# Linear attention, top-1 MoE and FFN in one kernel: the first expert unit's rows are all gathered in the attention's drain, and the last three chunks are routed inside that unit

## The chip, the cores and the metric

The kernel runs on one core of one Trainium2 chip. The metric is the device time of one execution in microseconds (us); lower is better. The names of the engines are those of the profile: PE (TensorE; PEld is its weight load), DVE (VectorE), ACT (ScalarE), POOL (GpSimd), and SP (SyncE, which issues most DMAs).

## What is computed

Three layers follow one another. The reference, cut:

```python
# q, k, v: (4, 8, 576, 64); w_phi: (64, 128)
proj = x @ w_phi;  proj -= max(abs(proj), -1);  phi(x) = concat(exp(proj), exp(-proj))
kv = phi(k).T @ v;  z = sum(phi(k));  attn = (phi(q) @ kv) / (phi(q) @ z + 1e-6)   # per head

x = attn as (2304 tokens, 512)
logits = x @ w_gate                         # 8 experts
e = argmax(logits);  g = max(softmax(logits))
# in token order, each expert takes its first 576 tokens (capacity); the rest are dropped
y[token] = g * (relu(x @ w1[e]) @ w2[e])    # w1: (512, 1024), w2: (1024, 512); 0 if dropped

h = y @ w_in                                # (512, 2048)
out = (h - tanh(h)) @ w_out                 # (2048, 512)
```

With the reference's inputs the counts of tokens per expert are 0, 576, 0, 0, 0, 0, 1152, 576, so three experts have work. In the first 1536 tokens they are 576 for expert 1 and 960 for expert 6.

## The kernel before

**Attention.** The 2304 tokens are 18 chunks of 128. One loop over steps s = 0..24 is a software pipeline: step s projects the k of chunk s, adds chunk s-1 to the sum kv (`kv_step`, L347), projects the q of chunk s-5 (`proj`, L304; `sub` at L312 and L315 takes the maximum off on DVE), transposes the q of chunk s-6 (`trans`, L381; ACT takes the exponentials) and multiplies it with kv (`num`, L420). From step 18 on there is no k left; steps 18 to 24 are called the drain here. Besides, w_in and the first part of w_out are unpacked piece by piece in steps 5 to 17 (`cv_*`: L94 on DVE, L98 and L278 on POOL).

**Routing** goes by groups of chunks. `route1` (14 short DVE operations, L448 to L489; the one-hot `oh` of each token's expert is L479) starts when the last chunk of a group has its `num`. `prefix` (PE, L502 to L505) counts the tokens of each expert ahead of each token. `route2` and `table` (DVE, L514 to L558) turn that into a slot per token, and `map_mm` (PE, L576) with `map_add` (L583) add the tokens to a table of slots. The first four groups of three chunks are "paced": their operations are spread over several steps between the large DVE operations of `sub`. The fifth group is (12, 13, 14), and the tail is (15, 16) and (17).

**The experts.** A unit is one expert with up to 576 tokens in six blocks of 96 rows; a row is fetched by an indirect DMA (`xgather`, L862), multiplied by its scale on POOL (`weigh`, L873), transposed on PE and split into a high and a low part (`xsplit`, L882; split at L850 on ACT and L851 on DVE). Every product is three matmuls (high x high, high x low, low x high; L854, L855, L856). A unit has an FF1 phase (eight steps `ff1` -> `relu` -> `ff2`, whose weights come through three raw buffers and are split at L836 on ACT and L841 on DVE) and an FFIN phase (sixteen steps `ffin` -> `gate` -> `ffout`). The result of ff2 is in four PSUM tiles `acc0` to `acc3` and is split into xh, xl by `evac_y`; `ff1` and `ffin` write two tiles `h0` and `h1` in turn. The last six pieces of w_out are unpacked inside unit 0 (`late_load`, `late_bits`, `late_split`): four in its FF1 phase (LF = 4), two in its FFIN phase. Units follow one another in nested branches on the number of experts in use.

**Between the two.** `first_gather` stands ahead of the last-but-one `num`: it finishes the table for 15 chunks, takes the first expert that has a token as unit 0 and gathers its first three blocks as far as these 15 chunks hold them. The last three chunks are not gathered. After the loop they are added by matmuls: `block_rows` (L621) puts the three gathered blocks into four PSUM banks, `block_add` (L627) adds the tokens of chunks 15 to 17 that belong there by a selection matrix (L535), and `x0` splits the four banks into xh and xl. The tail's rows are stored, its table is added, and the three other blocks are gathered when unit 0 begins. All work is issued in the order of the program (a manual schedule): each engine runs its instructions in that order, and an instruction that waits holds those behind it.

## Time and profile before

| | |
|---|---|
| time of three runs | 719.15 us median (717.67 to 719.91) |
| the profiled execution | 717.26 us, of which the span from first to last instruction is 715.4 us |
| mean granted clock of PE | 0.976 of full speed |
| busy share of the span | PE 92%, DVE 75%, ACT 60%, POOL 36% |
| drain's end to unit 0's first matmul | 192.91 to 216.35 us: 23.44 us, PE 14.44 us busy, clock 0.72 |
| FF1 phase of unit 0 | 216.35 to 267.80 us: 51.45 us, PE 50.80 us busy |
| the rest (unit 0's FFIN, two more units) | 267.80 to 715.40 us: 447.6 us, PE 428.79 us busy |

The table of stages is to be read by the difference between a stretch and PE's busy time in it: where the two agree, PE sets the time, and where they don't, a wait does. The granted clock is the share of full speed that TensorE had; a matmul takes about twice as long at 0.50.

### The profile page before, as it was taken

The page shows a single profiled execution, that of the slowest core. Times are in us where ns is not written, and L with a number is a line of the kernel's source. Part 1 is how long each engine was busy: PE and PEld are TensorE (multiplying, and loading weights), DVE is VectorE, ACT ScalarE, POOL GpSimd, SP SyncE. Part 2 cuts the span into 40 slices and gives each one's busy share as a digit, 9 for nine tenths or more (in the row PEclk, how much of TensorE's full clock was granted, in tenths as well). Part 3 has the DMA queues.
Part 4 walks back from the last instruction along what each step waited for, and adds up shares of the span by engine and source line. Part 5 has one row for each costly group of instructions (what it writes and reads, how often), then busy time and mean ns, then how long its engine had stood idle before and what let it go on. Part 6 is the DMA issues. An engine that isn't in the chain of part 4 may idle for free.

```text
span 715.4 us, 17537 instructions
## 1 busy us (share of the span) xinstructions
PE 656.8 (92%) x7148; PEld 636.5 (89%) x7148; DVE 537.2 (75%) x830; ACT 431.1 (60%) x735; POOL 256.4 (36%) x227
## 2 busy tenths in 40 slices
PE   7899788897679999989999999999999999999984
PEld 6789778787569998989999999999999999999983
DVE  4689898988757685888986554788987655788982
ACT  3599887874543675756764444656764544666661
POOL 1044544552224141563362011363462011362461
PEclk9999999998968999999999999999999999999998
DMA  7978677737616650120222550010222550010211
GB/s 179 278 232 286 205 234 228 247 108 212 199 56 191 225 191 1 30 78 1 74 72 68 176 167 20 1 34 1 79 67 91 168 156 15 2 35 1 68 36 37
DMA packets 62155, 81.35 MB, mean 114 GB/s; under 512 B 25792, under 2 KB 35136, under 8 KB 60400
## 3 DMA queue, kind: packets, MB, share of 16 engines
q1 hardware_dynamic: 58736, 71.92, 32.5%
q0 software_dynamic: 2624, 8.13, 4.0%
q8 instruction: 58, 0.95, 0.5%
q14 instruction: 33, 0.27, 0.1%
q10 hardware_dynamic: 704, 0.08, 0.1%
HBM read 67.06 MB, written 13.05 MB: 112 GB/s over the span
## 4 chain that ended last, share of the span: by engine, by line
PE 61%; DVE 16%; DMA 10%; ACT 7%; issue 3%; POOL 2%; SPq 0%; ACTq 0%; DVEq 0%; POOLq 0%
PE h L854 9%; PE acc L855 9%; PE acc L856 9%; PE acc L854 9%; PE h L856 9%; PE h L855 9%; DMA out<-row,ids 6%; DVE d L315 3%; DVE m L312 3%; PE xb L304 2%; PE kvb L347 1%; DMA raw<-win 1%; PE kvb L420 1%; POOL w_in_l L278 1%; ACT a L85 1%
## 5 line engine op out<-in xcount | busy, mean ns | idle before, releaser
L944 POOL TENSOR_SCALAR al<-ut 128x576 fp32r<-128x576 f32 (+1 forms) x51 | 83.0, 1627 | 148.9 <-ACT ut L940 107.6
L854 PE MATMUL h<-xh,w_in_h 128*128 128x288 f32 x384 | 115.0, 299 | 1.4 <-ACT ut L940 1.4
L855 PE MATMUL h<-xl,w_in_h 128*128 128x288 f32 x384 | 113.3, 295 | 0.0
L856 PE MATMUL h<-xh,w_in_l 128*128 128x288 f32 x384 | 113.0, 294 | 0.0
L841 DVE TENSOR_TENSOR w<-raw,w 128x512 fp32r<-128x512 f32 x98 | 68.0, 712 | 41.0 <-ACT w L836 36.5
L836 ACT CAST w<-raw 128x512 fp32r<-128x512 f32 x98 | 59.1, 620 | 53.6 <-DMA raw<-w 22.6
L939 ACT COPY hs<-h 128x576 f32<-128x576 f32 (+1 forms) x51 | 31.3, 614 | 94.5 <-DVE th L955 63.8
L854 PEld LDWEIGHTS h<-xh,w_in_h 128*128 128x128 f32 x384 | 72.0, 188 | 1.5 <-ACT ut L940 1.5
L854 PE MATMUL acc<-ah,w_oa_h 128*128 128x288 f32 x240 | 71.0, 296 | 2.0 <-ACT ah L931 2.0
L855 PE MATMUL acc<-al,w_oa_h 128*128 128x288 f32 x240 | 71.1, 296 | 1.6 <-DVE al L932 1.6
L856 PEld LDWEIGHTS h<-xh,w_in_l 128*128 128x128 f32 x384 | 72.3, 188 | 0.0
L855 PEld LDWEIGHTS h<-xl,w_in_h 128*128 128x128 f32 x384 | 72.1, 188 | 0.0
L856 PE MATMUL acc<-ah,w_oa_l 128*128 128x288 f32 x240 | 70.7, 294 | 0.0
L932 DVE TENSOR_TENSOR al<-y,ah 128x576 fp32r<-128x576 f32 (+1 forms) x51 | 41.3, 810 | 33.8 <-ACT ah L931 30.3
L984 POOL DMA_INDIRECT out<-row,ids x18 | 21.2, 1180 | 119.9 <-DVE row L982 69.7
L854 PE MATMUL h<-xh,w 128*128 128x288 f32 x192 | 58.7, 306 | 1.1 <-DVE al L900 1.1
L312 DVE TENSOR_REDUCE m<-xb 128x8 f32<-128x1024 f32 x33 | 40.2, 1219 | 24.2 <-PE xb L304 24.1
L855 PE MATMUL h<-xl,w 128*128 128x288 f32 x192 | 57.3, 299 | 0.0
L856 PE MATMUL h<-xh,w 128*128 128x288 f32 x192 | 57.2, 298 | 0.0
L854 PE MATMUL acc<-ah,w 128*128 128x288 f32 x192 | 56.7, 295 | 0.0
L856 PE MATMUL acc<-ah,w 128*128 128x288 f32 x192 | 56.6, 295 | 0.0
L855 PE MATMUL acc<-al,w 128*128 128x288 f32 x192 | 56.5, 294 | 0.0
(223 smaller groups left out, 1901.9 us busy)
## 6 DMA issues: line engine op xcount, KB each, us to landing
raw<-w SPq DMA_DIRECT2D x98, 256.0 KB, 3.0
raw<-win SPq DMA_DIRECT2D x8, 1024.0 KB, 7.0
raw<-wout SPq DMA_DIRECT2D x5, 1024.0 KB, 5.4
k<-kT SPq DMA_DIRECT2D x18, 256.0 KB
vt<-vT SPq DMA_DIRECT2D x18, 256.0 KB, 6.0
q<-qT SPq DMA_DIRECT2D x18, 256.0 KB, 6.1
out<-zero SPq DMA_DIRECT2D x18, 256.0 KB, 3.6
v<-v SPq DMA_DIRECT2D x16, 256.0 KB, 5.4
```

Source lines behind the costliest of these rows:

```text
L304: nc.tensor.matmul(ps[:, g, hp * DF:(hp + 1) * DF], src[64 * g:64 * g + 64, hp * P:(hp + 1) * P], wphi[64 * g:64 * g + 64], start=(hp == 0 ...
L312: nc.vector.tensor_reduce(out=m, in_=ps, axis=AX.X, op=ALU.max, apply_absolute_value=True)
L315: nc.vector.tensor_tensor(out=t, in0=ps, in1=m.unsqueeze(2).to_broadcast([P, H, DF]), op=ALU.subtract)
L836: nc.scalar.copy(d[:, 0], t)
L841: eng.tensor_tensor(out=d[:, 1], in0=t, in1=d[:, 0].bitcast(F32), op=ALU.subtract)
L854: nc.tensor.matmul(o, ah, bh, start=first, stop=False, skip_group_check=True)
L855: nc.tensor.matmul(o, ah, bl, start=False, stop=False, skip_group_check=True)
L856: nc.tensor.matmul(o, al, bh, start=False, stop=last, skip_group_check=True)
L932: nc.vector.tensor_tensor(out=AL[a][:, i], in0=y2[:, i], in1=AH[a][:, i].bitcast(F32), op=ALU.subtract)
L939: nc.scalar.copy(hs[:, i], h[:, i, 0:BLK])
L944: nc.gpsimd.tensor_scalar(out=AL[a][:, i], in0=ut[:, i], scalar1=C2, scalar2=None, op0=ALU.is_gt)
L984: ins = nc.gpsimd.indirect_dma_start(out=out[:, :], out_offset=bass.IndirectOffsetOnAxis(ap=ids[j % 2][0:RCH, rc:rc + 1], axis=0), in_=r[0 ...
```

## The change

- All groups have three chunks. Three are paced, the tail is (15, 16, 17). The group (9, 10, 11) is called `known`: its whole `route1` stands at step 17 in one piece, its `prefix` at step 18 ahead of `kv_step(17)`, its `table` in step 18.
- `first_gather` moves from step 23 to step 19. It chooses as unit 0 the expert with the most tokens in the first 12 chunks (`first_unit`, eight DVE operations in place of four; `had` keeps that count, at most 576). Its blocks 0 to 2 are gathered, weighed, and split by `xsplit` through PSUM bank `kvb[:, 2]` in steps 21 to 23, three weight pieces are split there too, and blocks 3 to 5 are gathered there. `block_rows`, `block_add`, `x0` and the matrix L535 are gone. `ff1(0)` follows the last `num`.
- The tail's `route1`, `prefix`, `route2`, `table`, `map_mm` and the list of the other units (`rest_units`) run inside unit 0, in its steps 0 to 3.
- At the end of unit 0's FF1 phase, `settle` compares the tokens that the chosen expert got in the end with `had` (`more1`). If more came, a branch gathers the six blocks again and repeats FF1 (`redo`); else nothing is done. With the counts above, `had` and the final count both meet the cap of 576.
- PSUM has the same tiles in the whole program: `acc` is the three banks of `kvb`, one tile, and `sb`; `ff1` and `ffin` write `xb` and `yb` in turn.
- Three late pieces of w_out stand in unit 0's FF1 phase and three in its FFIN phase (LF = 3, LO = 4). The four extra weight transfers into unit 0's free buffers are gone.

The diff, cut to its core:

```diff
-    NL = 3
+    NK = 12
+    sb = psp.tile([P, 512], F32, name="sb")
+    kvb = psp.tile([P, 3, 512], F32, name="kvb")
+    xb, yb = (psp.tile([P, 2, 512], F32, name=n) for n in ("xb", "yb"))
+    acc = [kvb[:, 0], kvb[:, 1], kvb[:, 2], sb]
+    hp_ = [xb, yb]
...
-        groups = [tuple(range(c, c + 3)) for c in range(0, NCH - NL, 3)] + [(NCH - 3, NCH - 2), (NCH - 1,)]
-        tailg = groups[-2:]
-        paced = groups[:4]
+        groups = [tuple(range(c, c + 3)) for c in range(0, NCH, 3)]
+        known, tailg = groups[NK // 3 - 1], groups[-1]
+        paced = groups[:3]
...
         def first_gather():
-            map_mm(maps[-1])
-            for _ in itertools.chain(map_add(maps[-1]), map_ids(), first_unit()):
-                pass
-            mo["first"]()
+            map_mm(known)
+            count_mm()
+            run(map_add(known), map_ids(), first_unit())
+            mo["first"](uroom)
...
-            if jn == NCH - 2:
+            if s == SK:
                 first_gather()
...
+            if s >= SK:
+                mo["drain"](s - SK)
+        tail = [lambda: rgen.update(t=route1(tailg)), lambda: run(itertools.islice(rgen["t"], 5)),
+                lambda: run(rgen["t"]), lambda: prefix(tailg, False),
+                lambda: (run(route2(tailg), table(tailg)), flush()),
+                lambda: (map_mm(tailg, False), count_mm(False)),
+                lambda: run(map_add(tailg), map_ids(), rest_units())]
...
-        LF = 4
-        LO = 3
+        LF = 3
+        LO = 4
...
+            if j == 0:
+                settle(aq[n1 - 1])
...
+        def settle(last):
+            with tc.If(nact[1] > 0):
+                redo(last)
...
+        def drain(s):
+            if s in (1, 2, 3):
+                weigh()
+                wcast()
+                wfetch(*((1, 1), (1, 1), (0, 1))[s - 1])
+            if s in (2, 3, 4):
+                xsplit(s - 2, kvb[:, 2])
+                early(s + 1)
```

Three places show in the order of instructions what moved. The names are those of the program's tiles: `d` is q after `sub`, `kp` and `qp` are the exponentials of k and q, `kvs` the sum kv in SBUF, `oh` the one-hot, `idc` and `idd` the table of slots, `few` and `key` small vectors of the choice of the unit.

On PE in step 18, before:

```order
L381 MATMUL yb<-ident,d 128x128 x8
L347 MATMUL kvb<-v_157,kp 64x74 x32
L304 MATMUL xb<-wphi,q 128x128 x8
L420 MATMUL kvb<-kvs_165,qp 64x74 x32
L576 LDWEIGHTS ta
```

and now:

```order
L382 MATMUL yb<-ident,d 128x128 x8
L494 LDWEIGHTS tri
L494 MATMUL sb<-oh,tri 128x24
L496 LDWEIGHTS ones
L496 MATMUL sb<-oh,ones 128x16
L496 LDWEIGHTS ones
L496 MATMUL sb<-oh,ones 128x8
L497 LDWEIGHTS ones
L497 MATMUL sb<-cum,ones 128x24
L348 MATMUL kvb<-v_156,kp 64x74 x32
L305 MATMUL xb<-wphi,q 128x128 x8
L423 MATMUL kvb<-kvs_164,qp 64x74 x32
```

The prefix of chunks 9 to 11, which waits for DVE's `oh`, now stands between the transposes of q and the last `kv_step`.

On DVE between the `sub` of q chunk 13 and that of chunk 14, before:

```order
L315 TENSOR_TENSOR d<-xb,m 128x1024
L448 TENSOR_SCALAR r<-dl 128x24
L449 RECIPROCAL r<-r 128x24
L458 TENSOR_TENSOR lgx<-dl,r 128x192
L462 TENSOR_REDUCE lg<-lgx 128x24
L465 TENSOR_REDUCE mx<-lg 128x3
L468 TENSOR_TENSOR ls<-lg,mx 128x24
L312 TENSOR_REDUCE m<-xb 128x8
```

and now the last eleven of the 26 rows that stand there, with the `sub` behind them (ahead of them are one `idc`, the nine operations of `route2` and `table`, and five on `idc`, `idd` and `idt`):

```order
L595 SCALAR_TENSOR_TENSOR key<-sb,few 128x8
L597 TENSOR_REDUCE few<-key 128x1
L599 TENSOR_SCALAR few<-key,few 128x8
L601 TENSOR_TENSOR key<-few 128x8
L603 TENSOR_REDUCE few<-key 128x1
L605 TENSOR_SCALAR reg_69<-few 1x1
L607 TENSOR_SCALAR few<-few 128x1
L610 TENSOR_SCALAR few<-few 128x1
L125 TENSOR_SCALAR few<-few 128x8
L127 TENSOR_TENSOR uroom<-idt,few 96x48
L130 TENSOR_REDUCE ids_72<-uroom 96x6
L313 TENSOR_REDUCE m<-xb 128x8
```

Six operations of `route1` stood there; now the whole choice of the unit does, behind a table that itself waits for PE.

On PE at the start of unit 0, before (`h_3137` is the first of the two h tiles):

```order
L576 MATMUL sb<-tb,ta 96x98
L780 LDWEIGHTS ones
L780 MATMUL sb<-cum,ones 128x8
L854 MATMUL h_3137<-xh_2500,w_0_2504 128x288
L855 MATMUL h_3137<-xl_2501,w_0_2504 128x288
L856 MATMUL h_3137<-xh_2500,w_0_2504 128x288
```

and now, from the last three `num` and `xsplit` on:

```order
L423 MATMUL kvb<-kvs_165,qp 64x74 x32
L868 MATMUL kvb<-ident,row_2545 128x96 x4
L423 MATMUL xb<-kvs_165,qp 64x74 x32
L840 MATMUL yb<-xh_2533,w_0_2537 128x288
...
L842 MATMUL yb<-xh_2533,w_1_2538 128x288
L868 MATMUL xb<-ident,row_2543 128x96 x4
L840 MATMUL yb<-xh_2533,w_2_2539 128x288
```

The first matmul of the unit follows the last `num`, and the second `ff1` (the last row) writes the tile yb that the first one wrote, since the `xsplit` between them takes xb.

## Rows read from the trace of the kernel before

**Rows 1.** Windows by stage: length, then busy us (and instructions) by engine, clock.
```profile
192.91:216.35 23.44, 14.44 (x58) 11.52 (x58) 12.87 (x50) 11.62 (x38) 6.67 (x11) 0.72 0.37 117
216.35:267.80 51.45, 50.80 (x372) 50.51 (x372) 37.54 (x71) 29.85 (x58) 18.06 (x18) 0.96 0.62 198
```

**Rows 2.** Timeline of PE, drain to unit: start, duration, line, operation, idle before.
```profile
155.24 2.27 PE L347 MATMUL kvb<-v,kp 128*64 128x74 f32 x64
...
167.11 1.94 PE L381 MATMUL yb<-ident,d 128*128 128x128 f32 x8 [3.68 <-DVE d L315]
...
174.03 1.09 PE L381 MATMUL yb<-ident,d 128*128 128x128 f32 x8
...
181.60 1.16 PE L304 MATMUL xb<-wphi,q 64*128 64x128 f32 x16
...
214.81 0.40 PE L576 MATMUL sb<-tb,ta 128*96 128x98 bf16 x2 [3.88 <-DVE ta L558]
...
216.35 0.59 PE L854 MATMUL h<-xh,w 128*128 128x288 f32 x1
...
220.10 0.43 PE L854 MATMUL h<-xh,w 128*128 128x288 f32 x1
```

**Rows 3.** Timeline of POOL in step 18, the unpacking beside route1.
```profile
157.19 2.14 POOL L98 TENSOR_TENSOR a<-a,m 128x1024 f32<-128x1024 f32 x1 [2.89 <-DVE a L94]
...
160.49 2.36 POOL L278 TENSOR_TENSOR w_oa_l<-a,w_oa_h 128x1024 fp32r<-128x1024 f32 x1 [0.52 <-ACT w_oa_h L275]
```

**Rows 4.** Timeline of DVE in the drain.
```profile
158.65 1.23 DVE L312 TENSOR_REDUCE m<-xb 128x8 f32<-128x1024 f32 x1 [1.54 <-PE xb L304]
...
161.05 1.83 DVE L448 TENSOR_SCALAR r<-dl 128x24 f32<-128x24 f32 x1
...
164.49 1.22 DVE L312 TENSOR_REDUCE m<-xb 128x8 f32<-128x1024 f32 x1
...
178.76 0.18 DVE L448 TENSOR_SCALAR r<-dl 128x24 f32<-128x24 f32 x1
...
181.19 0.18 DVE L479 TENSOR_TENSOR oh<-e,mx 128x24 bf16<-128x24 f32 x1
...
185.38 0.17 DVE L514 TENSOR_TENSOR pos<-sb,oh 128x24 f32<-128x24 f32 x1
...
187.46 0.46 DVE L558 TENSOR_TENSOR ta<-slot,pt 128x288 bf16<-128x288 f32 x1
188.36 0.25 DVE L583 TENSOR_TENSOR idc<-idc,sb 96x98 f32<-96x98 f32 x1 [0.44 <-PE sb L650]
...
190.53 0.20 DVE L122 TENSOR_REDUCE ids<-uroom 96x6 int32<-96x48 f32 x1
```

**Rows 5.** Timeline of unit 0's FF1 phase: DVE's relu part, PE's only wait.
```profile
222.37 0.76 DVE L900 SCALAR_TENSOR_TENSOR al<-h,ah 128x576 fp32r<-128x576 f32 x1 [1.45 <-ACT ah L899]
...
235.34 0.52 PE L882 MATMUL h<-ident,row 96*128 96x96 f32 x4 [0.65 <-issue]
```

**Rows 6.** Timeline of PE and DVE at the branch after the last unit.
```profile
696.44 0.37 PE L854 MATMUL acc<-ah,w_ob_h 128*128 128x288 f32 x1 [2.02 <-ACT th L946]
...
702.88 0.46 DVE L932 TENSOR_TENSOR al<-y,ah 128x288 fp32r<-128x288 f32 x1 [2.56 <-issue]
```

**Rows 7.** Timeline of PE's wait by a late piece of w_out in FFIN.
```profile
302.60 0.40 PE L855 MATMUL acc<-al,w_oa_h 128*128 128x288 f32 x1 [0.44 <-DVE al L932]
```

**Rows 8.** Timeline of a split of four PSUM banks: one tile (drain), four tiles (unit 0).
```profile
211.41 0.40 ACT L850 CAST xh<-kvb 128x288 fp32r<-128x288 f32 x1 [0.53 <-DVE xl L851]
...
277.81 1.56 DVE L851 TENSOR_TENSOR xl<-acc,xh 128x288 fp32r<-128x288 f32 x4
...
281.90 0.40 PE L854 MATMUL acc<-ah,w_oa_h 128*128 128x288 f32 x1 [0.95 <-ACT ah L931]
...
604.96 0.40 PE L854 MATMUL acc<-ah,w_oa_h 128*128 128x288 f32 x1 [0.49 <-ACT ah L931]
```

More of the change, by code (lines that the diff above doesn't have):

```diff
@@ L624, in block_add @@
-        def block_add(c):
-            for d in range(4):
-                nc.tensor.matmul(acc[d][:, 0:BLK], xt[c][:, d * P:(d + 1) * P], ohu[c],
-                                 start=False, stop=(c == NCH - 1), skip_group_check=True)
+            nc.vector.tensor_tensor(out=key, in0=one1, in1=wu, op=ALU.mult)
+            yield
+            nc.vector.tensor_reduce(out=reg1f, in_=key, axis=AX.X, op=ALU.max)
+            yield
+            nc.vector.tensor_scalar(out=reg1, in0=reg1f[0:1], scalar1=-1.0, scalar2=64.0, op0=ALU.mult, op1=ALU.add)
@@ L658, in flush @@
                 late.pop(0)()
-        for s in range(NCH + LAG + 2):
+        for s in range(LAST + 1):
             i, j, jt = s, s - LAG, s - LAG - 1
@@ L750, in attention @@
                                   in_=zero.unsqueeze(1).to_broadcast([P, 4, P]))
-            mo["after"](s)
-            if jn == NCH - 2:
-                xscale(NCH - 3)
-        prefix(tailg[0])
-        xscale(NCH - 2)
-        weave([], [route1(tailg[1]), route2(tailg[0])])
-        xscale(NCH - 1)
-        mo["highs"]()
-        block_rows(range(3))
-        block_add(NCH - 3)
-        prefix(tailg[1])
-        block_add(NCH - 2)
-        weave([], [route2(tailg[1])])
-        block_add(NCH - 1)
@@ L1189, in unit, with redo, piece @@
             return [aq2[n2 - 2], aq2[n2 - 1]]
+        def redo(last):
+            idload(0, hs[:, 0])
+            for rc in range(6):
+                xgather(0, rc)
+                weigh()
+                xsplit(rc)
+            spare = next(w for w in W2 if all(w is not x for x in w2q))
+            def piece(fc, half, d):
+                t = nxt("w", rawt)
+                wdma(0, fc, half, t)
+                wpend.pop()
+                nc.scalar.copy(d[:, 0], t)
+                nc.vector.tensor_tensor(out=d[:, 1], in0=t, in1=d[:, 0].bitcast(F32), op=ALU.subtract)
+                return d
+            pend = list(w2q)
+            for b, p in [(b, p) for b in range(2) for p in range(NP1)]:
+                for i in range(2):
+                    w1q.append(piece(2 * p + i, 0, W1[i]))
+                h = ff1(b)
+                if (b, p) == (1, NP1 - 1):
+                    relu(h, last)
+                    break
+                a = relu(h, 1 - last)
+                for i in range(2):
+                    w = piece(2 * p + i, 1, spare)
+                    for d in range(4):
+                        mm3(acc[d][:, 0:BLK], w[:, 0, d * P:(d + 1) * P], w[:, 1, d * P:(d + 1) * P],
+                            AH[a][:, i, :], AL[a][:, i, :], p == 0 and i == 0, p == NP1 - 1 and i == 1)
+                if p == NP1 - 1:
+                    evac_y(b)
+            assert pend == w2q and not w1q and not wpend
+        def settle(last):
+            if G > 1:
+                redo(last)
+                return
+            with tc.If(nact[1] > 0):
+                redo(last)
         def chain(j, prev):
@@ L1211, in after, with first @@
                     nc.gpsimd.memset(r[0:RCH], 0.0)
-        def first():
+        def first(room):
+            for r in rows:
+                nc.gpsimd.memset(r[0:RCH], 0.0)
             use(0)
-            idload(0, mo["room"])
+            idload(0, room)
             wfetch(0, 3)
             for rc in range(3):
-                xgather(0, rc, False, NT - NL * P)
-            weigh(3)
-        def highs():
-            for _ in range(3):
-                wcast_high()
-        def beside():
-            for half in (1, 1, 0):
-                wcast_low()
-                wfetch(half, 1)
@@ L1230, in x0 @@
-        def x0(acc):
-            for d in range(4):
-                split(xh[0][:, d, :], xl[0][:, d, :], acc[d][:, 0:BLK])
-        mo.update(beside=beside, highs=highs, alloc=alloc, after=after, first=first, x0=x0)
-        attention()
-        psp = ctx.enter_context(tc.tile_pool(name="psp", bufs=1, space=bass.MemoryType.PSUM, reuse_waits="tile"))
-        acc = [psp.tile([P, 512], F32, name=f"acc{i}") for i in range(4)]
-        hp_ = [psp.tile([P, 2, 512], F32, name=f"h{i}") for i in range(2)]
@@ L1266, in experts @@
+        mo.update(alloc=alloc, first=first, drain=drain)
+        attention()
+        mq = ctx.enter_context(tc.tile_pool(name="mq", bufs=1, side="right"))
+        W2 += [mq.tile([P, 2, 512], F32R, name=f"w2_{i}") for i in range(NW)]
+        AH += [mq.tile([P, 2, BLK], F32R, name=f"ah{i}") for i in range(2)]
+        AL += [mq.tile([P, 2, BLK], F32R, name=f"al{i}") for i in range(2)]
+        lord = list(range(NOA, 16))
+        tail = mo["tail"]
         chain(0, None)
```

308 lines of the change are left out of this document (143 added, 165 removed).

## The prediction

> **What bounds the kernel now.** I read the windows by stage first. In unit 0's FF1 phase PE is busy 50.80 of 51.45 us [rows 1]: PE sets the time there, and a wait that the change adds is paid in full. The one stretch with room is the 23.44 us from the last `num` to the first unit matmul: PE is busy 14.44 us in it, and the clock is 0.72 [rows 1]. So I read PE's timeline next, for what it waits for: POOL's weighed rows, then DVE's table, and around these waits the same operation takes 1.94 us where it takes 1.09 elsewhere [rows 2]. A wait of 3.68 or 3.88 us is followed by half clock (1.2 GHz); one of 2.02 us at the end of the program was not [rows 2, 6]. Then I read DVE and POOL in the drain, because the change moves the choice of the expert up to where these two decide, and last the branch, the late pieces and the split of PSUM, which the change touches in places where PE is the bound.
>
> **The gain: 23.44 us vanish, but the drain grows.** `block_rows`, `block_add`, `x0` and the wait for the table are gone, and `ff1(0)` follows the last `num`. If nothing else moved, this would be worth nearly the 23.44 us. I walk what now stands ahead.
>
> Step 18. The `prefix` of chunks 9 to 11 stands ahead of `kv_step(17)`, which began at 155.24 [rows 2], and needs `oh`. `route1` can't begin before DVE's unpacking ends, just as POOL's L98 starts at 157.19 and runs 2.14 us [rows 3]. From the first operation of `route1` to the end of `oh` it takes 181.19 + 0.18 - 178.76 = 2.6 us [rows 4]. That first operation is 0.18 us alone, but took 1.83 us from 161.05 while POOL's L278 ran from 160.49 for 2.36 [rows 3, 4]: held by POOL, it ends at 159.3 and `oh` at 159.33 + 2.43 = 161.8; free, `oh` ends at 159.9. I take 161.8, as the row with the same two operations side by side shows it. PE waits over 4 us, more than the 3.68 that cost the clock, so `kv_step` takes 2.27 x 1.94 / 1.09 = 4.0 us. With 0.2 for the prefix (my estimate from seven short matmuls' place in the drain) and 1.16 for `proj` [rows 2], `sub` of q chunk 13 begins at 161.8 + 0.2 + 4.0 + 1.16 = 167.2, and not at 158.65.
>
> Step 19. `sub` takes 161.05 - 158.65 = 2.4 us; one `idc` (0.25) and `route2` with `table` (185.38 to 187.92, 2.54) follow, then 0.44 of waiting for PE's map, then the chain from L583 to L122, 190.73 - 188.36 = 2.37 us for twelve operations, with four more at 0.2 each: 3.2 us [rows 4]. `sub` of chunk 14 begins at 167.2 + 2.4 + 2.8 + 0.4 + 3.2 = 176.0, and not at 164.49 [rows 4]: 11.5 us later. `trans` of chunk 15 moves from 174.03 to 185.5. From there the drain took 192.91 - 174.03 = 18.9 us, and nothing in it goes away. The three new `xsplit` use the bank tile `kvb` of `num`: two of them must be read by ACT and DVE (about 0.5 us each, by the 0.52 of PE's part [rows 5] and the 0.40 + 0.53 of a pair [rows 8]) before the next `num` writes. I take 2.5 us for them, between 0.5 (PE's transposes alone) and 3.5. So `ff1(0)` begins at 185.5 + 18.9 + 2.5 = 206.9 in place of 216.35: **-9.4 us**. The bounds: with POOL out of the way and full clock, sub of 13 begins at 163.6, the shift is 7.9, less some 1.7 for the half-clock `trans` and `proj` that step 20 has now (0.85 each, by the 1.94 and 1.09), and `ff1(0)` begins at 199.6 to 202; with every wait at its worst, at 209.
>
> **The clock at the unit's start.** 16 matmuls from 216.35 to 220.10 took 0.234 us each; the other 356 of the phase took (50.80 - 3.75) / 356 = 0.132 [rows 1, 2]. PE now comes in busy from `num`: 16 x 0.102 = **-1.6 us**.
>
> **FF1 phase of unit 0.** The tail's prefix, map and count add 0.7 us of PE (prefix 0.2, map and count 0.5). The second register load behind the branch costs as much as the first, 0.65 us with issue as its cause [rows 5]. The second `ff1` writes yb, which `relu(0)` has yet to read: about 0.65 us on ACT and 0.76 on DVE [rows 5], with one `xsplit` of 0.52 beside it: 0.9 us if DVE is free. It isn't: the tail's `route1` stands ahead of it (its first five operations, about half of the 2.6 us to `oh`). The third and fourth `ff1` write yb again, with an `ff2` between as cover (24 matmuls x 0.132 = 3.2 us), while DVE has route2, table, map and the list of units, about 8 us of short operations that did not stand in this phase. Bounds 1.5 (the first wait and part of one other) to 4.1; I take 3.0. Together **+4.35 us**.
>
> **The branch.** `settle` isn't there now, so the nearest rows are the branch not taken behind the last unit: PE stood 2.02 us, DVE 2.56 us [rows 6]. In the new one all engines jump over the body and then once more to its end, and PE's `ffin(0)` waits for ACT's and DVE's jump. The body isn't entered, because the chosen expert (6) has 960 tokens in 12 chunks and its cap is 576. Low bound 2.0 (PE's jump alone, second jump free), high 4.5 (two jumps each); I take **+3.3 us**, nearer to DVE's 2.56 with a hand-over than to two full jumps. On PE nothing covers it.
>
> **One more late piece in FFIN.** The steps of `gate` are as long as PE's, so POOL's work on a piece shows: PE waited 0.44 us once in the second piece [rows 7]. Bounds 0.4 and 2.3 (a wait of that size in each of five steps); I take **+1.2 us**. The piece taken out of the FF1 phase gains nothing, as PE didn't wait there.
>
> **The split of `acc`.** Now four PSUM tiles: ACT runs ahead and DVE's four take 1.56 us in a row [rows 8]. With three banks in one tile, ACT's next waits for DVE: 0.40 + 0.53 a pair [rows 8]. From DVE's first to its last that is 0.46 + 2 x 0.93 + 0.4 = 2.7 us, 1.1 us more. At the start of each unit's FFIN this stands between the gate of `ffin(0)` and that of `ffin(1)`, and PE already waits there (0.95 in unit 0, 0.49 in unit 2 [rows 8]), so it is paid in full: 3 x 1.1 = 3.3, and 0.5 at the program's end for the same reason: **+3.8 us**.
>
> **The sum.** -9.4 - 1.6 + 4.35 + 3.3 + 1.2 + 3.8 = +1.65 us. On the profiled 717.26 that is 718.9; on the median of 719.15, which the three runs give with 2.2 us between their ends, 720.8. I predict **720.8 us**: the hole between attention and experts closes by 11 us, and a slower drain, the branch and shared PSUM tiles take it back.
>
> **The rivals.**
> (a) Faster. One mechanism: `route1` in step 18 isn't held by POOL, so the drain keeps its clock. Then `ff1(0)` begins at 202, worth -14.35 - 1.6; with the branch at its low bound (2.0), 3.6 in FF1, 0.4 and 3.8 it is -6.1: 713.0 us. It decides from about `oh` before 160.5. For it: the first operation of `route1` might be issued before POOL's L98. Against: they start within 0.1 us of each other.
> (b) No change, by a cheap branch. The two engines with short bodies, DVE and ACT (the redo body has about 50 rows on DVE, some 370 on PE), don't stand at all, and PE stands 2.02: 1.3 us less, 719.5 us. For it: the body that is skipped now behind the last unit is a whole chain of units on every engine, so the 2.56 is from a far jump. Against: nothing in this trace has a near jump.
> The Trainium skill ("Runtime: NRT & Kernel Launch", section "Instruction fetch mechanics") says that a taken branch stalls when its target lies outside the window of instructions already fetched. By that rule (b) holds for DVE and ACT, and the time is that of (b); no run so far shows it.
> (c) Slower: the branch costs the clock. If PE's stand at the branch comes near the 3.58 to 3.88 that did so, 16 or more matmuls of `ffin(0)` run at half: branch 4.5, clock 1.6, FF1 at 5.45, late piece 2.3, evacuation 3.8, against -7.35 - 1.6: +8.7, 727.9 us. It decides from a stand of about 3.6 us.
> (d) The redo is entered after all. It repeats eight `ff1` and seven `ff2`, at least the 51.45 us of the phase [rows 1]: over 770 us. The counts speak against it.
>
> **How the numbers follow.** My forecast has 0.44 (its own range 718 to 725), (a) 0.31, (b) 0.11, (c) 0.12, (d) 0.02. Low and high are 712.0 and 728.0: the low end leaves out the part of (a) below 712, the high end the upper half of (c) and (d), together some 0.17. About 0.3% (2.15 us) is what can be told from no change, so same is 717.0 to 721.3. Of the forecast 0.20 lies there and 0.24 above; with (b), 0.08 is same and 0.03 slower. Faster 0.31, same 0.28, slower 0.41.
>
> **What would show it.** Right: PE's wait for `oh` at 155 to 162 and half clock behind it; the choice of the unit on DVE ending about 176; the first unit matmul at 205 to 209 at full clock; a stand of 2.5 to 4 us of PE ahead of unit 0's FFIN; pairs of 0.93 us at each evacuation. Wrong: a first unit matmul before 203, no stand at the branch, FF1 steps without waits, or an FFIN start that is no later in units 1 and 2 than now. The largest unknowns are the drain (7 us between its bounds) and FF1's waits.

## The result, and the profile after

The changed kernel takes 727.24 us (median of 4 runs, 726.52 to 729.08) against 718.41 us before: ratio 1.0125, 95% interval 1.0096 to 1.0153. It is 8.8 us slower. 720.8 us was forecast; the measured time lies inside the range and near its upper end, close to what rival (c) gave, though not by its mechanism.

The profiled execution is 729.08 us with a span of 727.3 us, 11.9 us more than the profiled one before; it is the slowest of the four executions, and the profiled one before (717.26 us) was faster than each of the four that the median before is from. By stage (from the first PE matmul of each phase to that of the next):

| stage | before | after | difference | forecast |
|---|---|---|---|---|
| program start to unit 0's first matmul | 216.35 | 210.83 | -5.5 | -9.4 |
| FF1 of unit 0, branch and clock included | 51.7 | 57.9 | +6.2 | +6.05 |
| FFIN of unit 0 | 109.7 | 112.6 | +2.8 | +2.3 |
| FF1 of unit 1 | 54.6 | 54.9 | +0.3 | 0 |
| FFIN of unit 1 | 105.9 | 108.1 | +2.1 | +1.1 |
| FF1 of unit 2 | 53.3 | 54.9 | +1.6 | 0 |
| FFIN of unit 2 up to the matmul behind the last branch | 104.9 | 109.3 | +4.4 | +1.1 |
| from there to the end | 19.0 | 18.9 | -0.1 | +0.5 |

The hole between attention and experts did close: the first unit matmul follows the last `num` without a gap. But unit 0 begins only 5.5 us earlier. Part of that was there before the drain: the projection of q chunk 12 in step 17, up to which PE runs the same operations in the same order in both kernels, began 1.64 us later in this execution than in the one before. The same row of PE before and after:

```profile
149.80 1.16 PE L304 MATMUL xb<-wphi,q 64*128 64x128 f32 x16 [0.52 <-DVE d L315]
```
```profile
151.44 1.16 PE L305 MATMUL xb<-wphi,q 64*128 64x128 f32 x16 [0.52 <-DVE d L316]
```

From this row to unit 0's first matmul it is 66.55 us before and 59.39 us after. PE's timeline of the drain (columns as in [rows 2]):

```profile
157.91 0.34 PE L559 MATMUL sb<-tb,ta 128*96 128x98 bf16 x3 [1.99 <-DVE ta L538]
...
163.16 0.18 PE L494 MATMUL sb<-oh,tri 128*128 128x24 bf16 x1 [3.83 <-DVE oh L471]
...
163.35 4.22 PE L348 MATMUL kvb<-v,kp 128*64 128x74 f32 x64
...
180.79 1.94 PE L382 MATMUL yb<-ident,d 128*128 128x128 f32 x8 [4.76 <-DVE d L316]
...
187.58 1.09 PE L382 MATMUL yb<-ident,d 128*128 128x128 f32 x8
...
203.56 3.73 PE L423 MATMUL kvb<-kvs,qp 128*64 128x74 f32 x64 [0.73 <-DVE xl L837]
208.14 0.52 PE L868 MATMUL kvb<-ident,row 96*128 96x96 f32 x4 [0.85 <-issue]
208.59 2.32 PE L423 MATMUL xb<-kvs,qp 128*64 128x74 f32 x64
210.83 0.40 PE L840 MATMUL yb<-xh,w 128*128 128x288 f32 x1
```

The walk of the prediction is there: the wait for `oh`, `kv_step(17)` at half clock (4.22 us; 4.0 forecast, 2.27 before in [rows 2]), then the wait for the choice of the unit ahead of q chunk 14. What the walk did not have is the first row, a wait of 1.99 us for the table of chunks 6 to 8. It lies ahead of the wait for `oh`, so the time up to `oh` is not longer by it. POOL and DVE in step 18:

```profile
159.07 2.12 POOL L106 TENSOR_TENSOR a<-a,m 128x1024 f32<-128x1024 f32 x1 [1.73 <-DVE a L102]
```
```profile
159.45 1.95 DVE L450 TENSOR_TENSOR lgx<-dl,r 128x192 f32<-128x192 f32 x1
...
178.17 1.21 DVE L313 TENSOR_REDUCE m<-xb 128x8 f32<-128x1024 f32 x1
```

POOL held `route1` as forecast, but at its third operation and not its first. `sub` of q chunk 14 begins at 178.17 (176.0 forecast); 1.64 of these 2.2 us are the later start of step 17.

In unit 0's FF1 phase PE waits once, and then runs at half clock for some 6 us. PE's timeline, and a window behind the wait (columns as in [rows 1]; a window counts every matmul that it touches):

```profile
217.49 0.61 PE L840 MATMUL yb<-xh,w 128*128 128x288 f32 x1 [2.86 <-DVE al L887]
...
223.66 0.31 PE L841 MATMUL kvb<-al,w 128*128 128x288 f32 x1
```
```profile
218.00:220.00 2.00, 2.00 (x10) 2.00 (x9) 1.90 (x7) 1.61 (x3) 0.00 (x0) 0.50 0.19 50
```

Between the starts of these two rows PE ran 25 matmuls in 6.17 us; at 0.132 us each they take 3.3 us, so 2.9 us were lost. The 1.6 us of clock that the new start saves are given back, and more, 6 us later. On DVE the subtraction that PE waits for stood behind the tail's `route1` and three weight pieces:

```profile
214.87 1.90 DVE L827 TENSOR_TENSOR w<-raw,w 128x512 fp32r<-128x512 f32 x3
216.69 0.75 DVE L887 SCALAR_TENSOR_TENSOR al<-yb,ah 128x576 fp32r<-128x576 f32 x1
```

At the branch (L1216), PE, DVE and ACT:

```profile
268.70 0.37 PE L840 MATMUL xb<-xh,w_in_h 128*128 128x288 f32 x1 [2.51 <-DVEq L1216]
```
```profile
267.15 1.34 DVE L827 TENSOR_TENSOR w<-raw,w 128x512 fp32r<-128x512 f32 x1 [1.85 <-ACTq L1216]
```
```profile
265.99 0.62 ACT L110 CAST w_ob_h<-hs 128x512 fp32r<-128x512 f32 x1 [2.22 <-POOL hs L106]
```

At the start of the three FFIN phases (the rows that answer to [rows 8]), with ACT's turn-taking in unit 0 and the clock in unit 1:

```profile
278.74 0.40 ACT L836 CAST xh<-kvb 128x288 fp32r<-128x288 f32 x1 [3.02 <-DVE xl L837]
```
```profile
283.45 0.40 PE L840 MATMUL kvb<-ah,w_oa_h 128*128 128x288 f32 x1 [1.82 <-ACT ah L918]
...
450.67 0.40 PE L840 MATMUL kvb<-ah,w_oa_h 128*128 128x288 f32 x1 [1.66 <-ACT ah L918]
...
613.63 0.40 PE L840 MATMUL kvb<-ah,w_oa_h 128*128 128x288 f32 x1 [1.64 <-ACT ah L918]
```
```profile
452.00:454.00 2.00, 2.00 (x12) 2.00 (x11) 1.79 (x4) 0.80 (x2) 0.00 (x0) 0.59 0.00 0
454.00:456.00 2.00, 2.00 (x10) 2.00 (x10) 1.29 (x2) 1.43 (x3) 0.00 (x0) 0.55 0.00 0
```

The wait is 0.9 to 1.15 us longer than before in each unit, as forecast. In units 0 and 1 it also costs the clock, which was not forecast: in unit 1, 14 matmuls from 452.37 to 455.72 took 1.5 us more than at 0.132 us each. In unit 2 the clock stayed at 1.00. Later in unit 0's FFIN phase PE waits for a row of the next unit, which POOL weighs behind the third late piece:

```profile
318.36 1.34 POOL L106 TENSOR_TENSOR raw<-raw,raw 128x512 f32<-128x512 f32 x1
```
```profile
323.17 0.55 PE L868 MATMUL xb<-ident,row 96*128 96x96 f32 x4 [1.81 <-POOL row L859]
...
331.58 0.52 PE L868 MATMUL xb<-ident,row 96*128 96x96 f32 x4 [1.49 <-issue]
```

And at the last branch, where PE stood 2.02 us before [rows 6], it now stands 5.39 us, with half clock behind it (0.53 from 708 to 712 us):

```profile
708.41 0.61 PE L840 MATMUL kvb<-ah,w_ob_h 128*128 128x288 f32 x1 [5.39 <-issue]
```

This branch is not part of the change. Before the change PE waited once more a few matmuls behind it, 1.83 us at 703.40; that wait is gone, which about pays for the half clock.

### The profile page after: what moved, and what is told of

It reads as the page before. It is cut to its first block, busy times and chain, and to the rows that moved or that the text cites. A ratio compares the mean times of both kernels' runs of the same rounds, so it can differ in the third digit from the quotient of the medians.

```text
span 727.3 us, 17438 instructions
## 1 busy us (share of the span) xinstructions
PE 657.5 (90%) x7111; PEld 638.0 (88%) x7111; DVE 532.6 (73%) x804; ACT 423.9 (58%) x705; POOL 258.4 (36%) x225
## 4 chain that ended last, share of the span: by engine, by line
PE 43%; DMA 7%; DVE 6%; ACT 4%; issue 1%; POOL 1%; DVEq 0%; ACTq 0%; POOLq 0%
DMA out<-row,ids 6%; PE kvb L841 6%; PE kvb L842 5%; PE kvb L840 5%; PE yb L841 4%; PE yb L840 4%; PE yb L842 3%; PE xb L840 3%; PE xb L842 3%; PE xb L841 3%; PE sb L840 2%; PE sb L841 2%; PE sb L842 2%; DVE al L919 1%; ACT hs L926 1%
## 5 line engine op out<-in xcount | busy, mean ns | idle before, releaser
L840 PE MATMUL yb<-xh,w_in_h 128*128 128x288 f32 x264 | 79.1, 300 | 0.0
L841 PE MATMUL yb<-xl,w_in_h 128*128 128x288 f32 x264 | 78.0, 295 | 0.0
L842 PE MATMUL yb<-xh,w_in_l 128*128 128x288 f32 x264 | 77.9, 295 | 0.0
L840 PE MATMUL kvb<-ah,w_oa_h 128*128 128x288 f32 x180 | 54.2, 301 | 5.2 <-ACT ah L918 5.1
L841 PE MATMUL kvb<-al,w_oa_h 128*128 128x288 f32 x180 | 54.8, 304 | 1.2 <-DVE al L919 1.2
L842 PE MATMUL kvb<-ah,w_oa_l 128*128 128x288 f32 x180 | 54.2, 301 | 0.0
L348 PE MATMUL kvb<-v,kp 128*64 128x74 f32 x1280 | 49.0, 237 | 5.3 <-issue 3.6
L840 PEld LDWEIGHTS yb<-xh,w_in_h 128*128 128x128 f32 x264 | 49.7, 188 | 0.0
L842 PEld LDWEIGHTS yb<-xh,w_in_l 128*128 128x128 f32 x264 | 49.7, 188 | 0.0
L841 PEld LDWEIGHTS yb<-xl,w_in_h 128*128 128x128 f32 x264 | 49.7, 188 | 0.0
```

The source lines that it names most:

```text
L348: nc.tensor.matmul(kvb[64 * a:64 * a + 64, bank, col * NKV:col * NKV + VS], kp[i][:, 4 * g + hp, s, 64 * a:64 * a + 64], vt[:, 2 * hp + g, :],
L840: nc.tensor.matmul(o, ah, bh, start=first, stop=False, skip_group_check=True)
L841: nc.tensor.matmul(o, ah, bl, start=False, stop=False, skip_group_check=True)
L842: nc.tensor.matmul(o, al, bh, start=False, stop=last, skip_group_check=True)
```

## The experiments

All kernels of this section are the changed kernel with one or more edits, and are told by their median and their ratio to the kernel before, measured beside it. The changed kernel itself is at 1.0125. Since single executions of these kernels differ by some us, I read the profile's stages beside the medians. One measure of the drain is free of what comes ahead: from the projection of q chunk 12 in step 17 (L305) to unit 0's first matmul, 210.83 - 151.44 = 59.4 us in the changed kernel, and 57.1 to 59.4 in the seven kernels whose drain is the same.

### x1: without the branch

```diff
-            with tc.If(nact[1] > 0):
-                redo(last)
+            return
```

> The changed kernel without the branch behind unit 0's FF1 phase (with these inputs its body is never entered). Theory 1, the branch is paid on PE: the stand of 2.51 us ahead of unit 0's FFIN is gone and nothing takes its place, so some 2.5 us less than the changed kernel: 724.7 us. Theory 2, the wait moves on: PE comes 2.5 us earlier to the first ffout, which waits for ACT and DVE anyway (1.82 us there now); then that wait grows to about 4 us and the time is 726 to 727 us.

Measured: 725.2 us (723.06 to 728.38), ratio 1.0116, interval 1.0079 to 1.0153. The stand is gone: FF1 takes 54.2 us, not 57.9 with the branch, and FFIN of unit 0 is as long as it was (112.4 and 112.6 us). The wait does not move on, so theory 1 holds in the profile. FF1 without the branch and with it, the changed kernel second:

```profile
209.31:263.55 54.24, 51.34 (x384) 50.72 (x382) 41.23 (x90) 28.94 (x56) 11.02 (x13) 0.97 0.53 165
```
```profile
210.83:268.70 57.87, 52.50 (x384) 52.02 (x381) 43.10 (x91) 30.51 (x58) 12.25 (x14) 0.94 0.53 164
```

PE is idle 2.90 us in place of 5.37, which is the stand of 2.5 us; the other 1.2 us are PE's busy time, as the half clock behind the second `ff1` was shorter in this execution. The medians are 2 us apart.

### x2: four casts, then four subtractions

```diff
             for d in range(4):
-                split(xh[b][:, d, :], xl[b][:, d, :], acc[d][:, 0:BLK])
+                nc.scalar.copy(xh[b][:, d, :], acc[d][:, 0:BLK])
+            for d in range(4):
+                nc.vector.tensor_tensor(out=xl[b][:, d, :], in0=acc[d][:, 0:BLK],
+                                        in1=xh[b][:, d, :].bitcast(F32), op=ALU.subtract)
```

> The changed kernel with one difference: evac_y issues the four ACT casts of acc first and then DVE's four subtractions, so that the one kvb tile no longer makes them take turns. Theory 1: the turns cost 1.0 us of waiting at each unit's FFIN start (1.82, 1.66, 1.64 us where the kernel before had 0.95, 0.52, 0.49) and the half clock behind that wait costs another 1 us in each: 3 x 2 = 6 us less, 721 us, with the clock at 1.00 there. Theory 2: only the waits go and the clock falls as before: 3 us less, 724 us. Theory 3: the first ffout waits for the gate of ffin(0) and not for the split: no change.

Measured: 720.11 us (717.13 to 721.51), ratio 1.0021, interval 0.9998 to 1.0043: 7 us of the 8.8 are gone. ACT's casts no longer take turns, and the waits are those of before:

```profile
273.16 0.97 ACT L901 CAST xh<-kvb 128x288 fp32r<-128x288 f32 x3
```
```profile
280.15 0.40 PE L840 MATMUL kvb<-ah,w_oa_h 128*128 128x288 f32 x1 [0.70 <-ACT ah L921]
...
445.87 0.40 PE L840 MATMUL kvb<-ah,w_oa_h 128*128 128x288 f32 x1 [0.55 <-ACT ah L921]
...
606.29 0.40 PE L840 MATMUL kvb<-ah,w_oa_h 128*128 128x288 f32 x1 [0.53 <-ACT ah L921]
...
697.26 0.37 PE L840 MATMUL kvb<-ah,w_ob_h 128*128 128x288 f32 x1 [1.58 <-ACT y L933]
```
```profile
448.00:450.00 2.00, 2.00 (x18) 2.00 (x17) 1.86 (x4) 0.24 (x2) 0.00 (x0) 1.00 0.00 0
```

The clock stays at 1.00 behind the wait: FFIN of unit 1 is 105.8 us, as before the change. That is theory 1 for unit 1. Unit 0 gains 0.6 us only (112.0 us): there the clock falls later, behind a wait of 1.80 us for POOL's row (0.52 from 322 to 324 us). The last row of PE is a surprise: the stand at the last branch fell from 5.39 to 1.58 us, and the split has nothing to do with it. x9 and x10 below part the two, and by them the forecast of 721 us was met by luck.

### x3: another tile for the first `xsplit` of the unit

```diff
-                        xsplit(2 + s)
+                        xsplit(2 + s, kvb[:, 2] if j == 0 and s == 1 else None)
```

> The changed kernel with one difference: the first xsplit inside unit 0 goes through kvb[:, 2], so the second ff1 writes xb and not yb, and needn't wait for relu(0). Theory 1, the shared tile is the cause of the 2.86 us wait at the second ff1: this wait and the half clock of some 5 us behind it go, about 5 us less, 722 us. Theory 2, DVE's queue is the cause (three weight pieces and half a route1 stand ahead of relu(0) on DVE): the second ff1 then waits 0.5 to 1 us for its second weight piece and the first ff2 waits for al instead, and 1 to 2 us are left to gain, 725.5 us.

Measured: 728.38 us (726.32 to 730.24), ratio 1.0145, interval 1.0108 to 1.0182: no gain. The second `ff1` does not wait any more, but the first `ff2` does, for the subtraction that frees the bank, behind the same queue on DVE, and the clock falls there:

```profile
220.31 0.61 PE L840 MATMUL kvb<-ah,w 128*128 128x288 f32 x1 [2.38 <-DVE xl L837]
```

FF1 is 1.4 us shorter (56.5 us), but 1.1 us of that is a shorter half clock (PE busy 51.38 us in place of 52.50). Theory 2 in kind, without its 1 to 2 us: DVE's queue is the cause, the shared tile only says where it is paid.

### x4 and x5: the prefix later, and `route1` ahead of the unpacking

```diff
-                if since[cs] == 1 + 2 * (cs in paced):
+                if cs != known and since[cs] == 1 + 2 * (cs in paced):
...
             if qq:
                 proj("q", j, xb)
+            if since[known] == 1:
+                prefix(known)
```

> The changed kernel with one difference: the prefix of chunks 9 to 11 stands behind kv_step(17) and the projection of q chunk 13, not ahead of them. Theory 1, the place of the prefix is the cause: PE has no wait of 3.83 us and no half clock in step 18, the sub of q chunk 13 begins right behind route1 at 163.8 instead of 169.4, and unit 0 begins about 5 us earlier: 722 us. Theory 2, the choice of the unit on DVE is the bound and swallows it: the table waits for the prefix as before and unit 0 begins within 1 us of 210.8: 726 to 727 us.

Measured (x4): 726.33 us (723.43 to 726.54), ratio 1.0104, interval 1.0069 to 1.0139. Unit 0 begins at 205.76; the drain's measure is 54.0 us, 3.1 to 5.4 less. Theory 1 for the drain. The three waits there now:

```profile
163.52 0.17 PE L494 MATMUL sb<-oh,tri 128*128 128x24 bf16 x1 [0.75 <-DVE oh L471]
...
166.01 3.16 PE L423 MATMUL kvb<-kvs,qp 128*64 128x74 f32 x64 [2.24 <-ACT kvs L358]
...
177.56 1.94 PE L382 MATMUL yb<-ident,d 128*128 128x128 f32 x8 [4.77 <-DVE d L316]
```

The median moved by 0.9 us only, where the profile shows 4.1 us up to FF1's end in unit 2 and 2.6 us in the span; four runs that differ by 3 us do not settle more.

x5 moves the unpacking's second half (L102 on DVE, L106 on POOL) in step 17 behind `route1`:

```diff
-            for _ in bits:
-                pass
+            if since[known] != 0:
+                for _ in bits:
+                    pass
...
                     weave([], [route1(cs)])
+            for _ in bits:
+                pass
```

> The changed kernel with one difference: in step 17, route1 of chunks 9 to 11 is issued ahead of the unpacking's second DVE operation (L102) and so ahead of POOL's L106 that follows from it. Theory 1, POOL held route1: its third operation (1.95 us beside L106, 0.36 alone) takes 0.36, oh ends 2.6 us after the table's last operation, near 160.5, PE's wait of 3.83 us falls to about 1.3, the clock stays at 1.00, and kv_step(17) takes 2.3 us instead of 4.2; unit 0 begins 5 us earlier, near 206. Theory 2, it was not POOL but the operation itself: it takes 1.95 us again and only L102's 1.2 us are gained.

Measured: 724.99 us (722.36 to 729.94), ratio 1.0075, interval 1.0047 to 1.0102. The operation takes 0.36 us with POOL out of the way, and PE waits 0.71 us instead of 3.83:

```profile
158.59 0.36 DVE L450 TENSOR_TENSOR lgx<-dl,r 128x192 f32<-128x192 f32 x1
```
```profile
160.72 0.18 PE L494 MATMUL sb<-oh,tri 128*128 128x24 bf16 x1 [0.71 <-DVE oh L471]
...
160.91 4.21 PE L348 MATMUL kvb<-v,kp 128*64 128x74 f32 x64
```
```profile
158.00:160.00 2.00, 1.81 (x11) 1.56 (x12) 1.83 (x8) 0.04 (x1) 0.00 (x0) 0.67 0.01 4
```

Theory 1 for the hold: POOL was the cause. But `kv_step(17)` still took 4.21 us, not the expected 2.3: the clock fell all the same, already behind the wait of 1.99 us for the table. The drain's measure is 55.9 us, 1.2 to 3.5 less, not 5.

### x6: the choice of the unit behind the `sub` of q chunk 14

```diff
-            if s == SK:
-                first_gather()
...
                 for _ in sub("q", j):
                     pass
+            if s == SK:
+                first_gather()
```

> The changed kernel with one difference: the table's end, the choice of the unit and the gathers stand behind the sub of q chunk 14 and not ahead of it. Theory 1, that chain is what makes PE wait 4.76 us for q chunk 14 and lose the clock: the wait falls under 2 us, no half clock follows, unit 0 begins 4 to 5 us earlier, near 206, and the rows, gathered 2.5 us later, still come before their xsplit. Theory 2, the rows then come late: the first xsplit waits for POOL's weighed row, and unit 0 begins where it did, 210 to 211.

Measured: 729.25 us (726.34 to 730.14), ratio 1.0131, interval 1.0103 to 1.016. The wait of 4.76 us fell to 2.14 without half clock, and another took its place one chunk later:

```profile
185.32 2.08 PE L305 MATMUL xb<-wphi,q 64*128 64x128 f32 x16 [3.63 <-DMA q<-qT]
```

Neither theory had that. The drain's measure is 58.8 us, no less than elsewhere. SP reads the number of the unit into a register before it issues the weights, and the load of q chunk 16 stands behind that on SP; the later the choice, the later this load. Unit 0's rows were not late.

### x7 and x8: together

x7 is x1, x2, x3, x4 and x6 in one. x8 keeps the branch and takes x2, x3, x4, x5, x6 and one more edit, the first `relu` ahead of the three weight pieces and of the tail's `route1`:

```diff
                 if j == 0 and s == 0:
-                    tail["a"]()
+                    aq[s] = relu(h)
                     wcast(3)
                     wfetch(0, 1)
                     wfetch(1, 1)
-                    aq[s] = relu(h)
+                    tail["a"]()
```

> The changed kernel with the split of acc in the order of four casts and four subtractions, the first xsplit of the unit through kvb[:, 2], the prefix of chunks 9 to 11 behind kv_step(17), the choice of the unit behind the sub of q chunk 14, and without the branch. If the waits seen in the trace add up: 7 us of the split, 2.5 of the branch, 5 of the prefix, 4 of the choice, 1 of the tile, 19.5 us less than 727.2: 708 us. If those in the drain hide one another (both are waits of PE for DVE, whose work stays the same), 5 of these 9 us stay: 713 us. If DVE sets the pace of the drain and of FF1 alike, no better than the kernel before: 718 us.

> The changed kernel with its branch kept, and five changes of order: the split of acc as four casts and four subtractions, the prefix behind kv_step(17), route1 of chunks 9 to 11 ahead of the unpacking, the choice of the unit behind the sub of q chunk 14, the relu of the first ff1 ahead of the three weight pieces and the tail's route1, and the first xsplit of the unit through kvb[:, 2]. If the waits add up: 7 us of the split, 9 of the drain, 3 to 4 of FF1's start with its half clock: 707.5 to 709 us. If the drain's hide one another: 712 us. If the first ff2 then waits for its weights instead (the three pieces come later), 2 us more than that.

Measured: x7 717.29 us (715.23 to 721.63), ratio 0.9974, interval 0.9952 to 0.9997; x8 717.65 us (715.72 to 719.0), ratio 0.9976, interval 0.9956 to 0.9995. Both are a little faster than the kernel before, 9 to 10 us short of the sums in which the waits add up and 4 to 6 us short of those in which the drain's hide one another. The drain's measure is 59.5 and 58.2 us, no less than in the changed kernel: in both PE waits for q's DMA (4.18 and 2.98 us). In x8 the first `ff2` also waits 3.36 us for the bank of the `xsplit`.

```profile
219.50 0.61 PE L845 MATMUL kvb<-ah,w 128*128 128x288 f32 x1 [3.36 <-DVE xl L842]
```

### x9 and x10: the code eight instructions further

PE stood 4.9 to 5.5 us at the last branch in the changed kernel and in x3 to x6, and 1.5 to 2.2 in x1, x2, x7 and x8. By my count of the compiled code, which the profiles do not show, the first five have the same number of PE instructions ahead of that branch's target, and in x2 and x8 it lies eight instructions further. So x9 is the changed kernel with four warm-up matmuls more (eight instructions, at the program's start), and x10 is x2 with four fewer. The edit of x9 (x10 has 11 there):

```diff
-        warm(15)
+        warm(19)
```

> The changed kernel with four more of the warm-up matmuls at the program's start, which are eight PE instructions, and nothing else: all PE code behind them lies eight instructions further, where it lies in the kernels with the other split order. Theory 1, the place of the code decides how long PE stands at the last branch: 5.39 us there now (4.9 to 5.5 in all five profiles with this place) become 1.5 to 2.1, no half clock follows, and the time is 3 to 4.5 us less, 723 to 724 us. Theory 2, the order of the split decides it: the stand stays at 5 us and the time at 727.

> The kernel x2 (the split of acc as four casts and four subtractions) with two warm-up matmuls fewer... in all four fewer, eight PE instructions less, so that its code lies where that of the changed kernel lies. Theory 1, the place of the code decides: the stand at the last branch grows from 1.58 to some 5 us, 3 to 4.5 us more than x2, 723.5 to 724.5 us, and the rest of x2's gain (3 us) is the split's own. Theory 2: the stand stays at 1.6 us and the time at 720.

Measured: x9 727.87 us (726.25 to 731.03), ratio 1.0139, interval 1.0105 to 1.0174; x10 724.37 us (723.15 to 725.17), ratio 1.0094, interval 1.0069 to 1.0119. PE at the last branch, x9 and then x10:

```profile
707.46 0.37 PE L840 MATMUL kvb<-ah,w_ob_h 128*128 128x288 f32 x1 [1.54 <-ACT y L930]
```
```profile
701.23 0.61 PE L840 MATMUL kvb<-ah,w_ob_h 128*128 128x288 f32 x1 [4.89 <-issue]
```

The stand follows the place of the code in both directions: theory 1 for the stand. For the time it holds in x10 (4.3 us more than x2; 3.5 us of it in the profile's last FFIN phase and what follows), but not in x9, for which 723 to 724 us was expected. There that last part is 2.6 us shorter, but the new branch became dearer, a stand of 2.92 us and then half clock, so that the first `ffin` and the last `ff2` take 7.96 us where they took 6.42, and FF1 has 1.0 us of new stands of PE (0.76 and 0.21).

```profile
270.00 0.37 PE L840 MATMUL xb<-xh,w_in_h 128*128 128x288 f32 x1 [2.92 <-DVEq L1216]
```

So x2's 7 us are two things: by the medians 2.9 us are the split's own (x10 against the changed kernel, same place of the code by that count), and 4.3 us are the place of the code. The first figure is not sharp, as the two intervals overlap.

### x11: the late piece behind the branch

```diff
-                if j == 0 and s - LO - 1 in range(LF):
+                if j == 0 and s - LO - 1 in range(LF) and s < n1 - 1:
...
                 settle(aq[n1 - 1])
+                late_split(lord[n1 - LO - 2])
```

> The changed kernel with one difference: the last late piece that stands ahead of the branch (its ACT cast waits for POOL, and the last weight piece waits behind it on ACT) is finished behind the branch. Theory 1, the 2.51 us at the branch are that queue: DVE's last subtraction ends at 268.49 and PE starts at 268.70, so the jump itself is 0.2 us; without the piece the stand falls under 1 us, and the time by about 1.5 to 2 us, 725.5 us. Theory 2, the jump's own fetch is the price: the stand stays at 2 to 2.5 us and the time at 727.

Measured: 727.91 us (725.5 to 735.56), ratio 1.0118, interval 1.0091 to 1.0146. The stand at the branch fell to 1.66 us, no longer for DVE but in PE's own queue, and a second one followed:

```profile
271.92 0.37 PE L840 MATMUL xb<-xh,w_in_h 128*128 128x288 f32 x1 [1.66 <-PEq L1217]
...
275.64 0.40 PE L840 MATMUL xb<-xh,w_in_h 128*128 128x288 f32 x1 [1.10 <-issue]
```

Neither theory alone: the queue of POOL, ACT and DVE is what PE waits for in the changed kernel, and with that gone PE stands 1.66 and 1.10 us by itself. The time is no less than that of the changed kernel, as theory 2 had it: the branch does not get cheaper by moving the piece.

### x12: what beats both

x12 keeps the branch and takes x2, x4, x5, x6, the earlier `relu`, x11, and issues the load of q chunk 16 ahead of the choice of the unit:

```diff
             if s == SK:
+                ldq(j + 2)
                 first_gather()
...
-            if 0 <= j + 2 < NCH:
+            if 0 <= j + 2 < NCH and s != SK:
                 ldq(j + 2)
```

> The changed kernel with its branch and these changes of order: the split of acc as four casts and four subtractions, the prefix of chunks 9 to 11 behind kv_step(17), their route1 ahead of the unpacking, the choice of the unit behind the sub of q chunk 14 with the load of q chunk 16 issued ahead of it, the relu of the first ff1 ahead of the weight pieces and the tail's route1, and the last late piece behind the branch. If the waits of x8 for q (2.98 us), for the shared bank (3.36) and at the branch (1.63) go: 5 to 6 us less than x8's 717.65, 712 us. If the drain is held by DVE's work and its chain of sub and trans: unit 0 begins at 205 to 207 as in x8 and the time is 715 us.

Measured: 716.46 us (715.03 to 718.19, 12 runs), ratio 0.9974, interval 0.9958 to 0.999: above both expected times (712 and 715 us). It is 1.6 us faster than the kernel before in the same comparison (718.07) and 10.8 us faster than the changed kernel. Unit 0 begins at 203.50 us, the wait for q is gone, the drain's measure is 52.5 us. But FF1 takes 60.3 us, with a new wait at the third `ff1`, 8.6 more than in the kernel before, where unit 0 begins 12.9 us later; there most of the gain is spent:

```profile
220.55 0.61 PE L846 MATMUL yb<-xh,w 128*128 128x288 f32 x1 [4.67 <-DVE al L893]
```

## Why the prediction was right or wrong

**What bounds the kernel: right.** The hole of 23.44 us closed, and nearly every wait that the change added on PE was paid in full. That the time fell inside the range is in part luck: the sum was 6.4 us too low by the medians and 10 us by the profiles, and several terms met their size by other parts.

**The drain: right in kind, mis-sized by 2.3 us.** 206.9 was forecast for unit 0's first matmul, 210.83 came, outside the 205 to 209 that the prediction named as a sign of being right. Of these 3.9 us, 1.64 were there at step 17, where PE had run the same operations in both kernels: in steps ahead of it the clock fell for a few us in this execution (0.72 from 102 to 106 us) and not in the one before (1.00). Counted from the projection of q chunk 12, 57.1 us was forecast, 59.4 came, and 57.1 to 59.4 in all seven kernels with this drain. In this execution two parts are too small. `proj` behind `kv_step(17)` was taken at full clock (1.16 us) and took 1.89; `sub` of chunk 14 came 0.5 us late, counted from step 17. And the three `xsplit` cost 4.3 us (23.2 from `trans` of chunk 15 to the unit, in place of 18.9) and not 2.5: each stands 0.85 us; the profile names no cause, but ACT's copy of the `num` ahead ends 0.1 us before (207.45 us and 0.59 long, for the third), and the walk left that out; behind the second, a `num` lost the clock (3.73 us for 2.31). POOL's hold on `route1`, the half clock in step 18 and the chain of the choice came as forecast. The reason for that half clock did not hold: the prediction took a wait of over 3.6 us to be what costs the clock, but in x5 it fell behind 1.99 us.

**The clock at unit 0's start: right and void.** The first 24 matmuls ran at 0.13 us, then the wait for yb took the clock again.

**FF1: right in size (+6.2 for +6.05), by luck.** The forecast waits of 3.0 us became one wait of 2.86 us and a half clock of 2.9 us, which the sum had at nothing. Against that, the stand of 0.65 us [rows 5], which the prediction counted a second time for the new register load, does not appear at all, and the branch was cheaper. x3 shows that the tile which the prediction named is only where DVE's queue is paid.

**The branch: 2.5 us for 3.3, half right in cause.** The prediction put it to the jump. In the trace it is the queue ahead of the branch: POOL's late piece holds ACT, ACT the last weight piece, DVE subtracts it until 268.49, and PE starts at 268.70. x11 took the piece away, and 1.66 us of PE's own remained. Removing the branch took 2.5 us off PE's idle time (x1). Rival (b) priced it at 2.0, which is nearer than the forecast. It also had DVE and ACT add nothing, and PE does start 0.2 us after DVE's last operation. By the rule of the Trainium skill ("Runtime: NRT & Kernel Launch", "Instruction fetch mechanics") a taken branch stalls when its target is not in the window of fetched instructions. What the traces show of DVE and ACT agrees with that. For PE they show that the place of the code matters (1.5 to 5.6 us for the last branch, x9 and x10); whether its target lay outside the window no run here shows.

**The late piece in FFIN: right in size, another wait.** PE's waits behind the start of unit 0's FFIN add up to 2.27 us before (0.44, 0.17, 0.30 and 1.36) and 3.56 us after (0.26, 1.81 and 1.49): 1.3 us more for a forecast of 1.2. POOL's work on the third piece stands ahead of the next unit's row there. No run takes that piece away, so this cause is argued and not shown.

**The split of `acc`: right, mis-sized.** The waits grew by 0.87, 1.14 and 1.15 us for a forecast of 1.1 each. What was missing is the clock: in FFIN of unit 1 a wait of 1.66 us followed closely by one of 0.40 left PE at half clock, 1.5 us more. The prediction priced a lost clock behind the new branch alone, in rival (c).

**Not in the sum at all:** the stand at the last branch, +3.4 us. It is the largest single part of what the sum lacks, and by x9 and x10 it comes from where the code lies, not from what the change does. In FF1 of unit 2 (+1.6 us) PE did not wait for `relu` before the change and waits 0.96 us after it, while unit 1 has such a wait in both (1.07 and 0.97 us); that cause stays open.

Rival (c), slower by the lost clock, gave 727.9, which is close to the measured time; but its place, the new branch, kept the clock at 1.00 (windows of 264 to 274 us). The clock was lost at the second `ff1`, at the FFIN starts of units 0 and 1 and at the last branch. Rival (a) asked for `route1` free of POOL, with the clock kept; x5 freed it, the clock fell all the same, and it was worth 1.2 to 3.5 us and not 5 or more.

## What to carry to other kernels

When work moves ahead of a waiting engine, list every instruction that stands between the new producer and its consumer on each in-order queue, SP's too, and ask where the wait goes next: here it went from the table to the one-hot, from there to q's subtraction and then to q's DMA. Two engines that split one PSUM tile of several banks took turns here (0.92 us a pair); issue one engine's reads first, then the other's. A gain of a few us can be undone by where the code lies (4.3 us in x10): compare variants with the same number of instructions ahead of a branch. And before two profiles are compared stage by stage, look how far apart they are where the kernels are still the same (1.64 us here).

## What was not expected of the hardware

- The same branch cost PE 1.5 to 2.2 us or 4.9 to 5.6 us in the fourteen profiles here (seven each), by a shift of eight instructions of the code (x9 against the changed kernel, x10 against x2). In x1 and x7 the short stand (2.23 and 2.10 us) was followed by half clock (0.52 and 0.50), so that little was gained there.
- Short waits can cost the clock, but do not always. Two waits of 1.66 and 0.40 us, with 0.4 us of work between, were followed by half clock in unit 1 (0.59 and 0.55 in the windows of 452 to 456 us); 1.64 and 0.40 in unit 2 of the same execution were not (1.00 from 614 to 616), nor were 0.52 and 0.40 before the change, nor 2.02 [rows 6]. The wait of 1.99 us in step 18 was followed by half clock in x5 (0.67) and x12 (0.54), and in x4 it was not (1.00 from 158 to 160 us).
- Executions reached the same row of step 17 between 149.5 and 155.9 us (x8 and x11), some 6 us apart, before anything that differs between these kernels. Single executions of one kernel differed by 2.6 us (the changed kernel) to 10 us (x11).
